# Hash attention and an MLP mixer on one core: two hashes moved at the start of the first pair

## The chip, the core and the metric

One core of a Trainium2 chip. The metric is the device time of one execution in microseconds; a median is taken over the executions of a version. "Before" is the kernel as it was, "changed" the one with the diff below.

## The reference, cut to what matters

```python
q_bits = (np.einsum('bhsd,dk->bhsk', q, proj) > 0)       # 6 sign bits per query, k the same
mask = q_bucket[:, :, :, None] == k_bucket[:, :, None, :]
scores = np.where(mask, scale * np.matmul(q, k.transpose(0, 1, 3, 2)), -1e9)
attn = exp(scores - max) / (sum + 1e-9)
x = np.matmul(attn, v)                                     # 4 batches, 8 heads, 768 tokens, 64 columns
u = x + token_mlp(x)                                       # [cut]
out = u + channel_mlp(u)                                   # [cut]
```

Only the attention matters here. Heads are handled in pairs, 16 pairs in all, and each pair in two halves of 384 queries.

## The kernel before

The hash is a matmul of q or k with the projection, then a sign. Instead of masking, the kernel adds to each score a product of the sign bits that is zero where all bits agree and hugely negative where one differs. So each block of scores takes q and k matmuls first, then a bit product into the same buffer in PSUM (where this kernel's matmuls write), then an exponential on ScalarE. The score buffers are three, and the hash of the next pair borrows one of them.

```python
def hashes(n):                        # a later pair
    g = pool.tile([P, HALF], BF16, name="g", tag="g", bufs=2)
    ps = psum.tile([P, 2, 512], F32, name="hp", tag="sc", bufs=3)[:, 0]
    # [cut] four matmuls into ps
    nc.vector.tensor_scalar(g, ps[:, :HALF], 0.0, 0.5, op0=ALU.is_gt, op1=ALU.subtract)
    nc.scalar.mul(g, g, bitscale)
    # [cut] eight DMAs from g into bitrows[n % 2]

def first_hashes(which, half):        # the first pair: straight into its place, no DMA
    # [cut] sl: the half of the tokens; to: its place in bitrows[0]
    ps = psum.tile([P, 512], F32, name="hw", tag="sm" if which else "acc", bufs=1)[:, :HALF]
    nc.tensor.matmul(ps, projwide, loaded[0][0][:, which, sl], start=True, stop=True)
    nc.vector.tensor_scalar(to, ps, 0.0, 0.5, op0=ALU.is_gt, op1=ALU.subtract)
    if which:
        nc.vector.tensor_scalar(to, to, widescale, None, op0=ALU.mult)

# in scores(), for the first half of the first pair; GR = 3, NR = 6
for c in range(NR):
    sc = psum.tile([P, 2, 512], F32, name="sc", tag="sc", bufs=3)
    product(sc, qkt, c, True)
    if first and c < GR:
        waiting.append((c, sc))
        if c == GR - 1:
            first_hashes(1, 1)
            for c, sc in waiting:
                product(sc, bits, c, False)
            for c, sc in waiting:
                exponential(sc)
        continue
    product(sc, bits, c, False)
    exponential(sc)
```

At the very start TensorE runs idle matmuls on ones while the first data arrive (`for _ in range(14)`). The main loop:

```python
for n in range(len(pairs)):
    for half in range(2):
        now = Half(n, half)
        now.scores()
        if half == 0:
            add_values(n)             # ScalarE: sum of v over tokens, rows "vt"
        now.add(0)                    # VectorE: three sums of e, rows "esd"
        # [cut] row sums of the pair before
        if half == 0 and n + 1 < len(pairs):
            hashes(n + 1)
            load_qk(n + 2)
        # [cut]
        now.add(1)
        # [cut] a step of the weight conversion
        if before:
            before.weigh()            # TensorE: e times v, rows "acc"
```

## Time and profile before

| | before |
|---|---|
| median of the first three runs | 846.69 us (846.1 to 848.8) |
| span of the profiled execution | 844.8 us |
| TensorE busy | 835.2 us, 99% |
| first hash matmul starts | 4.89 us |
| first score matmul starts | 6.34 us |
| first weighted product ("acc") starts | 22.24 us |

A timeline row gives the start in us, the duration of the merged instructions, engine, source line, operation, output<-input, shapes and count; in brackets stands the idle time just before and what ended it. A row of waits gives engine and group that waited, what for, the total in us, the number of waits and the longest. Ends of matmuls are modelled, so distances from start to start are the safer measure. The distance from the first score matmul to the first weighted product is the ruler of this document: 22.24 - 6.34 = 15.90 us before. It spans everything that the change touches, and nothing of the start-up. Its rows, with the first hash:

```profile
4.89 1.53 PE L319 MATMUL hw<-qk,projs 128*128 128x384 f32 x4 [0.78 <-DMA qk<-in_qk]
6.34 2.21 PE L340 MATMUL sc<-qk 64*128 64x384 f32 x12
...
22.24 4.09 PE L388 MATMUL acc<-e,vn 128*64 128x384 f32 x24
```

The prediction shows the rows that matter. One more row of VectorE's timeline of before belongs to it, the first sum of the second pair, with the slack in front of it:

```profile
29.03 0.96 DVE L376 SCALAR_TENSOR_TENSOR esd<-e 128x768 f32<-128x768 f32 x1 [2.06 <-ACT e L347]
```

VectorE stood idle for 2.06 us until ScalarE had made the second pair's first exponentials. Whatever arrives earlier on TensorE and ScalarE has this much room before VectorE is in the way.

### The profile page before, as it was taken

Reading aid. Unit: us, or ns where it says so; the run is one execution under the profiler, and the core shown is the slowest. Engines: PE = TensorE matmul, PEld = TensorE weight load, DVE = VectorE, ACT = ScalarE, POOL = GpSimd, SP = SyncE. Lnnn points to the kernel's source line nnn. Section 1 sums busy time; section 2 is a strip of 40 time slices with the busy share of each in tenths; the row PEclk is TensorE's granted clock in tenths of the full one; section 3 lists DMA queues with packets and bytes.
Section 4 is the critical chain, followed back from the end, with each engine's and each line's share of the span. In section 5 each row is a group of like instructions: output and inputs, shape, how many; then the busy total and the mean of one; then the engine's idle time right before and its main releaser. Section 6 shows DMA issues by size and latency. Waiting matters only on the chain.

```text
span 844.8 us, 9068 instructions
## 1 busy us (share of the span) xinstructions
PE 835.2 (99%) x3449; PEld 384.8 (46%) x3449; DVE 532.3 (63%) x652; ACT 318.7 (38%) x492; POOL 52.0 (6%) x55
## 2 busy tenths in 40 slices
PE   8999999999999999999999999999999999999997
PEld 4444444444444444555444444444444444444444
DVE  4789898998988677796564674435365432336411
ACT  4787788887888772121112101011110002111000
POOL 1000000000000000000011102001110201001110
PEclk9999999999999999999999999999999999999999
DMA  4345354455523227631012101321211110000001
GB/s 154 120 135 183 137 154 138 162 177 165 152 78 116 78 81 206 230 119 38 0 38 74 37 29 35 137 86 38 75 37 62 38 67 9 0 0 1 25 26 53
DMA packets 48755, 73.74 MB, mean 87 GB/s; under 512 B 27769, under 2 KB 29505, under 8 KB 48705
## 3 DMA queue, kind: packets, MB, share of 16 engines
q1 hardware_dynamic: 48144, 72.49, 26.2%
q8 instruction: 29, 0.48, 0.2%
q10 hardware_dynamic: 560, 0.61, 0.2%
q14 instruction: 22, 0.17, 0.1%
HBM read 59.85 MB, written 12.58 MB: 86 GB/s over the span
## 4 chain that ended last, share of the span: by engine, by line
PE 98%; DVE 1%; DMA 0%; ACT 0%; issue 0%; DVEq 0%; ACTq 0%
PE b L691 51%; PE sc L340 19%; PE acc L388 15%; PE t L616 5%; PE t L635 5%; PE sums L412 1%; PE hp L301 1%; DMA qk<-in_qk 0%; PE hw L319 0%; DVE esd L380 0%; ACT e L347 0%; DVE esd L376 0%; ACT g L306 0%; DVE bits L321 0%; DVE u L777 0%
## 5 line engine op out<-in xcount | busy, mean ns | idle before, releaser
L340 PE MATMUL sc<-qk 64*128 64x384 f32 x768 | 158.6, 492 | 2.4 <-DVE g L305 1.5
L698 ACT COPY p<-b 128x512 f32<-128x512 f32 x72 | 42.2, 586 | 307.7 <-PE b L691 307.7
L347 ACT ACTIVATE e<-sc 128x768 f32<-128x768 f32 x192 | 152.9, 812 | 14.0 <-PE sc L340 13.2
L388 PE MATMUL acc<-e,vn 128*64 128x384 f32 x768 | 130.9, 490 | 0.0
L380 DVE TENSOR_TENSOR esd<-esd,e 128x768 f32<-128x768 f32 x128 | 122.3, 955 | 10.3 <-ACT e L347 0.5
L691 PE MATMUL b<-r,WC 128*128 128x512 f32 (+1 forms) x300 | 125.6, 575 | 0.0
L691 PE MATMUL b<-T,SW 128*128 128x512 f32 x216 | 96.6, 592 | 0.0
L340 PEld LDWEIGHTS sc<-qk 64*128 64x128 f32 x768 | 66.5, 187 | 58.1 <-issue 44.9
L691 PEld LDWEIGHTS b<-r,WC 128*128 128x128 f32 x300 | 57.0, 190 | 67.1 <-issue 63.6
L388 PEld LDWEIGHTS acc<-e,vn 128*64 128x64 f32 x768 | 52.3, 137 | 74.9 <-issue 74.3
L691 PE MATMUL b<-T,WC 128*128 128x512 f32 x144 | 67.7, 592 | 0.0
L721 DVE TENSOR_TENSOR r<-p,u 128x512 f32<-128x512 f32 x18 | 12.5, 692 | 86.5 <-ACT u L698 86.5
L691 PE MATMUL b<-XT,WC 128*128 128x512 f32 x144 | 64.7, 592 | 0.0
L691 PEld LDWEIGHTS b<-T,SW 128*128 128x128 f32 x216 | 41.0, 190 | 51.7 <-issue 50.0
L340 PE MATMUL sc<-bits 64*128 64x384 bf16 x384 | 62.9, 323 | 0.0
L691 PE MATMUL b<-r,SW 128*128 128x512 f32 x144 | 62.8, 592 | 0.0
L717 POOL TENSOR_TENSOR p<-p,p 128x512 f32<-128x512 f32 x18 | 22.8, 1267 | 639.2 <-ACT p L698 628.4
L698 ACT COPY u<-b 128x512 f32<-128x512 f32 x24 | 14.1, 586 | 79.1 <-PE b L691 79.1
L691 PEld LDWEIGHTS b<-T,WC 128*128 128x128 f32 x144 | 27.4, 190 | 34.4 <-issue 34.4
L691 PEld LDWEIGHTS b<-r,SW 128*128 128x128 f32 x144 | 27.4, 190 | 34.4 <-issue 34.0
L691 PEld LDWEIGHTS b<-XT,WC 128*128 128x128 f32 x144 | 27.3, 190 | 34.1 <-issue 33.8
L616 PE MATMUL t<-x,W 128*128 128x512 f32 x96 | 41.8, 593 | 0.0
(85 smaller groups left out, 755.2 us busy)
## 6 DMA issues: line engine op xcount, KB each, us to landing
raw<-in_moe_w_ch SPq DMA_DIRECT2D x16, 768.0 KB
seen<-in_qk SPq DMA_DIRECT2D x16, 768.0 KB
qk<-in_qk SPq DMA_DIRECT2D x15, 768.0 KB
vn<-in_v SPq DMA_DIRECT2D x16, 384.0 KB
vt<-in_vT SPq DMA_DIRECT2D x16, 384.0 KB
bounced<-stage SPq DMA_DIRECT2D x32, 192.0 KB
x<-bounced SPq DMA_DIRECT2D x4, 1536.0 KB
out<-p SPq DMA_DIRECT2D x18, 256.0 KB
```

Source lines behind the costliest of these rows:

```text
L301: nc.tensor.matmul(ps[32 * j : 32 * j + 32, :HALF], projblk, loaded[n][0][:, j % 2, sl], start=True, stop=True,)
L340: nc.tensor.matmul(sc[:, i, :HALF], t[rows, 1, P * c : P * c + P], t[rows, 0, qs], start=start, stop=not start,)
L347: nc.scalar.activation(e, sc[:, :, :HALF], ACT.Exp, scale=SCALE)
L380: nc.vector.tensor_tensor(self.d, self.d, e, op=ALU.add)
L388: nc.tensor.matmul(acc[D * i : D * i + D], vn[:, i, c], e[:, i], start=(c == 0), stop=(c == NR - 1),)
L412: nc.tensor.matmul(ps[at : at + 32], ones[:, :32], self.halves[h].d[:, i], start=True, stop=True,)
L616: nc.tensor.matmul(ps, W1[:, r, P * j : P * j + P], x[:, r], start=(r == 0), stop=(r == NR - 1),)
L635: nc.tensor.matmul(ps[:, :HALF], r1[:, j, P * cb : P * cb + P], W2[:, j, HALF * half : HALF * half + HALF], start=(j == 0), stop=(j == NJ ...
L691: nc.tensor.matmul(self.ps[i][:, cols], left(k), right(k)[:, cols], start=first and k == ks[0], stop=k == ks[-1], skip_group_check=True,)
L698: nc.scalar.copy(c, self.ps[i])
L717: nc.gpsimd.tensor_tensor(p7, p5, p7, op=ALU.add)
L721: nc.vector.tensor_tensor(r[:, 3], p7, u, op=ALU.add)
```

## The change

The first move lets the first exponentials start without waiting for a hash that only the fourth block needs. The second takes the second pair's hash, on VectorE and ScalarE, out from behind sums that nobody waits for yet.

```diff
                     if first and c < GR:
                         waiting.append((c, sc))
                         if c == GR - 1:
-                            first_hashes(1, 1)
                             for c, sc in waiting:
                                 product(sc, bits, c, False)
-                            for c, sc in waiting:
                                 exponential(sc)
+                            first_hashes(1, 1)
                         continue
@@
                 now.scores()
+                if half == n == 0:
+                    hashes(1)
                 if half == 0:
                     add_values(n)
@@
-                if half == 0 and n + 1 < len(pairs):
+                if half == 0 and 0 < n < len(pairs) - 1:
                     hashes(n + 1)
+                if half == 0:
                     load_qk(n + 2)
```

## The prediction

> **What bounds the kernel now.** I read the page first, for the engine that fills the span and for the slices in which it is not full; then the waits of the tensor engine alone, because they say how much there is to win; then the chain of waits and the timelines of TensorE, VectorE and ScalarE for the first 45 us, because all of the change runs there. The page says:
>
> ```profile
> PE 835.2 (99%) x3449; PEld 384.8 (46%) x3449; DVE 532.3 (63%) x652; ACT 318.7 (38%) x492; POOL 52.0 (6%) x55
> ...
> PE   8999999999999999999999999999999999999997
> ...
> PE 98%; DVE 1%; DMA 0%; ACT 0%; issue 0%; DVEq 0%; ACTq 0%
> ```
>
> TensorE carries 98% of the chain that ends last. Only the first and the last slice are below 9. The waits of TensorE over the whole execution are four rows:
>
> ```profile
> PE sc L340 <- DVE g L305: 1.5, 1, 1.5
> PE idle L450 <- DVE ones L97: 1.0, 1, 1.0
> PE sc L340 <- ACT e L347: 0.9, 2, 0.6
> PE hw L319 <- DMA qk<-in_qk: 0.8, 1, 0.8
> ```
>
> The second and fourth are the start-up before the first hash at 4.89 us and are not touched. The other two, 2.4 us in three places, all lie between 10 and 20 us; after that TensorE waits for nothing. Ends of matmuls are modelled, so I also measure these gaps from start to start. One block of scores (four matmuls on q and k, two on bits) is issued every 0.81 us when nothing holds it, as 11.48 to 12.29 shows below; its bit part takes 0.17 of that, from 12.12 to 12.29.
>
> ```profile
> 8.48 0.91 PE L319 MATMUL hw<-qk,projs 128*128 128x384 f32 x2
> 9.33 0.66 PE L340 MATMUL sc<-bits 64*128 64x384 bf16 x6
> 10.57 0.92 PE L340 MATMUL sc<-qk 64*128 64x384 f32 x4 [0.58 <-ACT e L347]
> 11.32 0.33 PE L340 MATMUL sc<-bits 64*128 64x384 bf16 x2
> 11.48 0.81 PE L340 MATMUL sc<-qk 64*128 64x384 f32 x4
> ...
> 12.12 0.33 PE L340 MATMUL sc<-bits 64*128 64x384 bf16 x2
> 12.29 0.81 PE L340 MATMUL sc<-qk 64*128 64x384 f32 x4
> ...
> 13.19 0.91 PE L319 MATMUL hw<-qk,projs 128*128 128x384 f32 x2
> 14.03 0.85 PE L301 MATMUL hp<-qk,projs 128*32 128x384 f32 x8
> 14.81 0.92 PE L340 MATMUL sc<-qk 64*128 64x384 f32 x4
> ...
> 18.21 0.92 PE L340 MATMUL sc<-qk 64*128 64x384 f32 x4 [1.51 <-DVE g L305]
> ...
> ```
>
> The issue gaps are then: 9.33 + 3 x 0.17 = 9.84 to 10.57, 0.73 us; 14.81 + 2 x 0.81 = 16.43 to 18.21, 1.78 us; 18.21 + 0.81 = 19.02 to the fourth block's 19.62, 0.60 us. Together 3.1 us, which no version of this change can exceed. The reason for the two later ones stands in the other two timelines:
>
> ```profile
> 14.61 0.95 DVE L376 SCALAR_TENSOR_TENSOR esd<-e 128x768 f32<-128x768 f32 x1
> 15.67 2.02 DVE L380 TENSOR_TENSOR esd<-esd,e 128x768 f32<-128x768 f32 x2
> 17.60 0.55 DVE L305 TENSOR_SCALAR g<-hp 128x384 bf16<-128x384 f32 x1
> ```
>
> ```profile
> 14.03 0.84 ACT L292 ACTIVATE vt<-vt 128x768 f32<-128x768 f32 x1
> ...
> 18.25 0.62 ACT L306 ACTIVATE g<-g,bitscale 128x384 bf16<-128x384 bf16 x1 [3.30 <-DVE g L305]
> 18.77 4.41 ACT L347 ACTIVATE e<-sc 128x768 f32<-128x768 f32 x6
> ```
>
> The second pair's sign step g sits on VectorE behind three additions of e (14.61 to 17.69), though its matmuls end near 14.9. Its PSUM tile is one of the three score buffers, so the third score block of half 1 cannot start until g has read it (18.21). ScalarE's scaling of g stands before the exponentials of half 1, so they start at 18.77 and the fourth score block, which needs the first one's buffer, at 19.62.
>
> [...] ScalarE stood still for 3.30 us before g while two finished score blocks were waiting for their exponentials. [...] The trace has 812 and 602 to 616; I use the trace's start-to-start times. [...] the largest here is 1.78 us and the clock granted is 1.00 in every stretch of the first 65 us, so I give the clock no share in the gain.
>
> **The change part by part.** No instruction is added or removed; two things move.
>
> *Part 1*, the second half of the key bits. Before, its matmuls (8.48, 0.85 us to the next start) hold up the first three bit products. Now these start at 8.48 and the hash follows at 8.48 + 0.51 = 8.99. The first exponential, 9.70 before, starts 0.85 earlier at 8.85, and the first buffer is free about 0.85 later, near 9.7. So the fourth block's q and k matmuls start when the hash is through, 8.99 + 0.85 = 9.84, no longer at 10.57. But its bit product needs the key bits of that late hash. VectorE took them 0.95 us after the start of the hash (8.48 to 9.43) and was done at 10.35, 1.87 after it. Now that is 8.99 + 1.87 = 10.86; with the 0.1 us that a wait for VectorE and the weights takes, the bit product starts near 10.96. Without a wait it would start at 9.84 + 0.64 = 10.48, so a new wait of 0.5 us appears. Against 11.32 the gain is 0.35 us, not the 0.73 of the gap removed. From there TensorE sets the pace (0.81 a block against 0.72 an exponential), so hash, second pair's hash and half 1 move by 0.35: 12.84, 13.68 and 14.46.
>
> *Part 2*, g ahead of the sums. The second pair's hash matmuls start at 13.68. VectorE can read them 0.89 us later (a later pair: matmuls at 31.98, g at 32.87), at 14.57, and is done at 15.12. ScalarE starts 0.10 later, as 18.15 to 18.25 did, at 15.22; the sum of vt follows after 0.52 (the distance from 18.25 to 18.77), at 15.74, and now lies between g and the exponentials instead of in ScalarE's idle time. It holds them up by 0.82 (32.13 to the next start at 32.95). So the exponentials of half 1 start at 16.56 rather than 18.77, 2.21 us sooner. The third block starts unhindered at 14.46 + 1.62 = 16.08, since g has read its buffer at 15.12; the fourth at 16.56 + 0.85 = 17.41, after a wait of 0.5 us. The gap of 1.78 is gone; that of 0.60 stays at 0.5.
>
> *Sum.* By start times: the first weighted product, 22.24 before, starts near 20.05. By gaps: 3.1 before, 0.5 + 0.5 after, 2.1 us won. I take 2.15 us, of which 0.35 is part 1 and 1.8 is part 2. Since TensorE waits for nothing from 20 us to the end, its earlier start should reach the end whole: 846.69 - 2.15 = 844.5 us.
>
> **The rivals.** (a) VectorE becomes the bound. Its sums of the first half now start near 15.1 instead of 14.61, and its backlog moves little: five additions per half take 5.1 us, so it is done with half 0 near 20.2, with half 1 near 25.4 and with the weight conversion's two steps (1.54 us) near 26.95. The second pair's first exponentials then ask for it at 29.03 - 2.2 = 26.85. Before, it sat idle for 2.06 us there; that slack is now spent to the last tenth. Against this rival: TensorE needs the sums of half 1 only near 29.2 (31.31 - 2.15), and later rows show VectorE idle again (0.8 us before g at 32.87). If I have missed a microsecond of VectorE work, up to 1 us is given back: 845.5. (b) The bits' transfers. The eight issues took 6.09 us from 18.89 and move with g to about 15.9, ending near 22.0; the second pair's first bit product moves only from 27.01 to 24.85. Its margin grows from 2.0 to 2.9 us. I see no new wait there. (c) The new wait in part 1 is longer than reckoned, say 0.9 instead of 0.5, and part 1 gains nothing: 844.9. If the wait is short and both remaining gaps shrink, 3.1 us is the most: 843.6. (d) The time saved is lost to a transfer that has a time of its own. The loads of the third pair stand behind the bits on the same queue and so come sooner as well; nothing speaks for this. All 2.15 us lost would be 846.7.
>
> **Range and chances.** Two thirds of the weight lie at 2.0 to 2.4 us of gain. The three runs before spread over 2.7 us (846.1 to 848.8), more than the whole effect, and skewed upward, so the range is mostly that of the runs: 843.4 to 846.3. A change of 2% would be 17 us; the gaps hold 3.1. Faster by over 2%: 0.01; within: 0.98; slower: 0.01, for an order that brings a wait into every pair, which I don't see since the later pairs keep theirs.
>
> **What would show it.** In the profile after: the wait of TensorE for g is gone from its list; a wait of about 0.5 us for the key bits (VectorE, widescale row) appears at the fourth block near 10.9; the exponentials of half 0 start near 8.85 and of half 1 near 16.6; ScalarE's 3.30 us idle before g shrinks to about 1.4; the fourth block of half 1 starts near 17.4, the first weighted product near 20.05; VectorE's 2.06 us idle before the second pair's sums is nearly gone, while the first conversion step starts almost where it did (25.4). The prediction is wrong if the first weighted product is well away from 20.05, or if it is there and a new TensorE wait after 20 us gives the gain back.

No term of the sum is cut: it comes to 0.35 + 1.8 = 2.15 us won, and 846.69 - 2.15 = 844.5 us, as it stands. 812 is the mean of one exponential over 768 columns and 602 to 616 the duration of g's scaling, both in ns and from the trace before; "the largest here" is the largest issue gap. The 0.1 us for a wait for VectorE is the author's estimate: in the trace before, TensorE and ScalarE started 0.06 and 0.10 us after g was done (18.15 to 18.21 and to 18.25).

## The result, and the profile after

The median was 845.91 us (844.12 to 846.87, six runs) against 847.53 us for the kernel before (846.04 to 848.80, six runs). The ratio is 0.9978, with a 95% interval of 0.996 to 0.9996; a ratio here is the mean time of one kernel's runs over that of the other's in the same rounds, so it is not quite the ratio of the medians. 844.5 was predicted with a range of 843.4 to 846.3. The profiled execution took 846.24 us, with a span of 844.5 us: only 0.3 less than before. At first sight the gain of 2.15 us is not there. First the waits of TensorE over the whole execution of the changed kernel:

```profile
PE idle L449 <- DVE ones L97: 1.0, 1, 1.0
PE hw L319 <- DMA qk<-in_qk: 0.7, 1, 0.7
PE sc L340 <- ACT e L347: 0.3, 1, 0.3
PE sc L340 <- DVE bits L323: 0.2, 1, 0.2
```

The wait of 1.5 us for g is gone, as foreseen, the waits for ScalarE have shrunk from 0.9 to 0.3, and the new wait for the key bits is there. There is none after 20 us. So the gaps closed, and yet the span hardly moved. TensorE's timeline in the same trace shows why:

```profile
4.91 2.90 PE L319 MATMUL hw<-qk,projs 128*128 128x384 f32 x4 [0.67 <-DMA qk<-in_qk]
7.74 3.09 PE L340 MATMUL sc<-qk 64*128 64x384 f32 x12
10.67 0.65 PE L340 MATMUL sc<-bits 64*128 64x384 bf16 x6
11.25 0.91 PE L319 MATMUL hw<-qk,projs 128*128 128x384 f32 x2
12.10 0.92 PE L340 MATMUL sc<-qk 64*128 64x384 f32 x4
13.17 0.34 PE L340 MATMUL sc<-bits 64*128 64x384 bf16 x2 [0.16 <-DVE bits L323]
...
19.66 0.92 PE L340 MATMUL sc<-qk 64*128 64x384 f32 x4 [0.29 <-ACT e L347]
...
22.29 4.09 PE L387 MATMUL acc<-e,vn 128*64 128x384 f32 x24
```

The first hash began at 4.91 us, as before (4.89), but its four matmuls took 2.83 us to the first score matmul instead of 1.45, and the twelve score matmuls and their first bit product followed 2.93 us later instead of some 2.1. The same instructions ran at half rate until somewhere near 9.6 us. From the first score matmul the first weighted product is 22.29 - 7.74 = 14.55 us away, 1.35 less than before even with half-rate matmuls in that stretch. Whether the half rate comes from the change or from the execution is the question for the experiments.

ScalarE's timeline of the same execution, to be held against the three rows of before in the prediction:

```profile
17.48 0.61 ACT L306 ACTIVATE g<-g,bitscale 128x384 bf16<-128x384 bf16 x1 [1.47 <-DVE g L305]
18.00 0.83 ACT L292 ACTIVATE vt<-vt 128x768 f32<-128x768 f32 x1
...
18.82 4.41 ACT L347 ACTIVATE e<-sc 128x768 f32<-128x768 f32 x6
```

ScalarE's idle time before g shrank from 3.30 to 1.47 us (about 1.4 predicted), and the sum of vt now stands between g and the exponentials and delays them by 18.82 - 18.00 = 0.82 us.

### The profile page after: what moved, and what is told of

Same layout as the page of the kernel before. It is cut to its first block, busy times and chain, and to the rows that moved or that the text cites. A ratio compares the mean times of both kernels' runs of the same rounds, so it can differ in the third digit from the quotient of the medians. Undisturbed runs are those within 1.5% of the kernel's fastest.

```text
span 844.5 us, 9070 instructions
## 1 busy us (share of the span) xinstructions
PE 837.3 (99%) x3449; PEld 385.9 (46%) x3449; DVE 532.4 (63%) x652; ACT 318.6 (38%) x492; POOL 51.8 (6%) x55
## 4 chain that ended last, share of the span: by engine, by line
PE 98%; DMA 0%; ACT 0%; DVE 0%; issue 0%; ACTq 0%
PE b L693 51%; PE sc L340 19%; PE acc L387 15%; PE t L618 5%; PE t L637 5%; PE sums L411 1%; PE hp L301 1%; PE hw L319 1%; DMA qk<-in_qk 0%; ACT vt L292 0%; ACT e L347 0%; ACT g L306 0%; DVE g L305 0%; DVE bits L321 0%; DVE u L779 0%
```

## The experiments

Twelve runs. Those with "16" have two more idle matmuls at the start, those with "one idle matmul" have thirteen fewer.

### 1. The changed kernel once more

No edit.

> The changed kernel itself, unchanged, timed again. Theory A (the two moves save about 2.1 us of TensorE gaps; apart from that each execution, of either kernel, starts its score matmuls with TensorE at full or at half rate by chance, worth about 2.2 us): the times of both kernels fall into two groups about 2.2 us apart, before near 846.2 and 848.5, changed near 844.3 and 846.3, and the lower groups differ by 1.8 to 2.3 us. Rival B (the change itself makes the half-rate start): the kernel before has no slow group of its own, or the changed kernel shows only half-rate starts. Rival C: the spread is smooth noise without groups.

Measured: 843.91, 844.23, 844.23, 844.31, 844.36 and 846.58 us; the kernel before in the same rounds 845.72 to 846.62 (four runs) and 848.06 to 848.83 (seven). TensorE's timeline of this execution:

```profile
4.87 1.53 PE L319 MATMUL hw<-qk,projs 128*128 128x384 f32 x4 [0.61 <-DMA qk<-in_qk]
6.32 2.21 PE L340 MATMUL sc<-qk 64*128 64x384 f32 x12
8.36 0.66 PE L340 MATMUL sc<-bits 64*128 64x384 bf16 x6
8.95 0.91 PE L319 MATMUL hw<-qk,projs 128*128 128x384 f32 x2
9.79 0.92 PE L340 MATMUL sc<-qk 64*128 64x384 f32 x4
10.87 0.34 PE L340 MATMUL sc<-bits 64*128 64x384 bf16 x2 [0.16 <-DVE bits L323]
...
17.36 0.92 PE L340 MATMUL sc<-qk 64*128 64x384 f32 x4 [0.29 <-ACT e L347]
...
19.98 4.09 PE L387 MATMUL acc<-e,vn 128*64 128x384 f32 x24
```

The same kernel, and now the first hash takes 1.45 us to the first score matmul. The ruler reads 19.98 - 6.32 = 13.66 us, 2.24 less than before. So the half-rate start belongs to the execution and not to the kernel: both kernels have fast-group and slow-group runs. Over all, 25 of 48 runs of the kernel before lie at 845.66 to 846.89 (mean 846.25) and 23 at 847.67 to 849.03 (mean 848.43). Of 12 runs of the changed kernel 7 lie at 843.91 to 844.52 (mean 844.24) and 5 at 845.62 to 846.87 (mean 846.30). Lower group against lower group the change is worth 2.0 us, upper against upper 2.1. The two medians of the first comparison mixed the groups in different shares (two of six lower runs after, three of six before), which is why they differ by 1.6 only.

### 2. Each move alone

```diff
 # part1: only the first move        # part2: only the second move
-first_hashes(1, 1)                  +if half == n == 0:
 products of bits, exponentials      +    hashes(1)
+first_hashes(1, 1)                   add_values(n), sums
```

> The first move alone: second half of the key bits hashed behind the first three bit products. Theory A: 0.35 us in the timeline (fourth block's bit product about 6.1 us after the start of the first hash in a full-rate start, where before has 6.43), and the gap before the third block of half 1 stays at 1.8 us; in time about 846 in the fast group. Rival: the new wait for the key bits eats all of it, 0.0 us.

> The second move alone: the second pair's sign step and scaling ahead of the sums. Theory A: 1.8 us in the timeline (first weighted product about 15.5 us after the start of the first hash in a full-rate start, where before has 17.35), no TensorE wait for g; fast group about 844.6. Rival: it depends on the first move and gives clearly less than 1.8, say 1.2.

| | first score matmul | first weighted product | ruler | gain | times |
|---|---|---|---|---|---|
| before | 6.34 | 22.24 | 15.90 | | |
| first move | 6.17 | 21.66 | 15.49 | 0.41 | 845.57 to 846.04, five runs |
| second move | 6.02 | 20.10 | 14.08 | 1.82 | 844.17 to 844.65 (four), 847.01, 847.02 |
| both | 6.32 | 19.98 | 13.66 | 2.24 | 843.91 to 844.52 (seven), 845.62 to 846.87 (five) |

0.41 + 1.82 = 2.23: the moves add up, and each is what the prediction gave it (0.35 and 1.8). The rivals (0.0 for the first, 1.2 for the second) fall. The expectation for the first move counted from the first hash, 6.1 us to the fourth block's bit product; that was 10.72 - 4.60 = 6.12.

### 3. What the half-rate start hangs on

```diff
-        for _ in range(14):
+        for _ in range(1):      # and range(16) in the runs with 16
             nc.tensor.matmul(idle[:D, :D], ones, ones, start=True, stop=True)
```

> The changed kernel with one idle matmul at the start instead of fourteen. Theory A: every execution starts at half rate, so there is one group only, no run near 844.3; the score matmuls of the first block take about twice as long from 4.9 us to at least 8 us, and the times lie [...] 846.0 to 847.7. Rival (the half-rate start has nothing to do with how long TensorE was busy before): the same two groups as the changed kernel, 844.3 and 846.3.

Changed kernel, one idle matmul: 845.51 to 846.58 us, five runs, none near 844.3. Two runs lie below the range expected, the lowest by 0.5; that range was the author's estimate. The hash took 2.83 us in the trace, and 3.11 us followed to the first bit product.

> The kernel before with one idle matmul instead of fourteen, so that it always starts at half rate, as the changed kernel with one did (845.51 to 846.58, median 846.13). Theory A: one group, 2.2 us above that, median near 848.3, the same as the slow group of the kernel before (848.0 to 848.9); in the trace the first hash's matmuls at 2.83 us to the first score matmul instead of 1.45, and from 12 us on the distances of the first profile. Rival (the slow group comes from somewhere else, such as a drop of the rate in the idle stretch of 1.8 us): times clearly above 849.5, or two groups again.

Kernel before, one idle matmul: 847.89, 848.07, 848.25, 848.33, and then 849.57 and 850.03. The first four are what theory A said, mean 848.14 against 846.08 of the changed kernel: 2.06 us, in executions that all have the short warm-up (the two profiles reach full rate at different times, though; the table below has 9.81 and 8.15 us). The last two are a miss, and the profiled execution was one of them (849.57). Its TensorE timeline, around the stretch that the change closes:

```profile
5.07 2.90 PE L319 MATMUL hw<-qk,projs 128*128 128x384 f32 x4 [3.59 <-DMA qk<-in_qk]
...
19.86 0.92 PE L340 MATMUL sc<-qk 64*128 64x384 f32 x4 [1.51 <-DVE g L305]
20.61 0.33 PE L340 MATMUL sc<-bits 64*128 64x384 bf16 x2
21.27 1.17 PE L340 MATMUL sc<-qk 64*128 64x384 f32 x4 [0.33 <-ACT e L347]
22.23 0.54 PE L340 MATMUL sc<-bits 64*128 64x384 bf16 x2
22.55 1.50 PE L340 MATMUL sc<-qk 64*128 64x384 f32 x4
23.83 0.54 PE L340 MATMUL sc<-bits 64*128 64x384 bf16 x2
```

And its stretches (columns after the stretch: its length, busy us and count of PE, PEld, DVE, ACT and POOL, then the granted clock, DMA share and GB/s):

```profile
15.00:20.00 5.00, 3.49 (x24) 1.30 (x26) 3.99 (x6) 1.71 (x4) 0.00 (x0) 1.00 0.00 0
20.00:25.00 5.00, 4.67 (x22) 2.32 (x24) 4.47 (x5) 4.03 (x6) 0.00 (x0) 0.68 0.03 8
```

From one bit product to the next it is 1.60 us (22.23 to 23.83), twice the 0.81 of full rate, and the granted clock is 0.68 on average from 20 to 25 us. So the rival named in the expectation is real too, though not the main thing: soon after TensorE had waited for 1.51 us and again for 0.33 (the brackets above), it fell back to half rate in this profiled run, and the time of the other run at 850.03 fits it.

> The changed kernel with 16 idle matmuls instead of 14. Theory A2: no run in the group near 846.4; all between 843.8 and 845.6, so about 2.2 us below the kernel before with 16. Rival: the two groups of the changed kernel, 844.3 and 846.4, remain.

> The kernel before with 16 idle matmuls at the start instead of 14. Theory A2 (in the traces so far TensorE was at full rate from its first score block where the pause between the idle matmuls and the first hash was 0.3 to 0.6 us long or the rate had changed before that pause, and at half rate until about 9.5 us where the pause was 0.67 us and nothing had changed before it): two more idle matmuls take 0.45 us, the pause shrinks to at most 0.35 us, and the slow group at 848.0 to 848.8 disappears; all runs lie between 845.7 and 847.8. Rival (the start-up rate is pure chance, whatever TensorE does before): as many runs near 848.4 as before, about half.

Changed kernel with 16: 843.59 to 844.48, five runs, no upper group. Kernel before with 16: 845.63 to 847.08, five runs, none in the upper group, though 847.08 lies between the two. The mean goes from 845.10 (12 runs with 14) to 844.03, and from 847.29 (48 runs) to 846.24. Both expectations held, but for the lowest runs, which lie 0.2 and 0.1 below the edges given. That chance alone kept ten runs in a row out of the upper groups is unlikely: with the shares of lower runs seen with 14 (7 of 12 and 25 of 48), about 1 in 400. The means mix different chips and rounds; against the kernel before in the same rounds, the ratio of the kernel before with 16 is 0.9987 (0.9973 to 1.0001), which is not clear of 1.

The packed trace keeps records of TensorE's clock, one for each change (no view of the profile prints them; their effect is in the clock column of a table of stretches). The first record of full rate in each profiled execution, and the pause between the last idle matmul and the first hash (as shown in the brackets of its row; none where it has no bracket):

| execution | idle matmuls | pause, us | full rate from, us | hash to first score matmul, us |
|---|---|---|---|---|
| before | 14 | 0.78 | 3.82 | 1.45 |
| second move alone | 14 | 0.41 | 3.90 | 1.46 |
| changed, again | 14 | 0.61 | 4.80 | 1.45 |
| first move alone | 14 | 0.34 | 4.85 | 1.57 |
| before, second look | 14 | 0.51 | 6.23 | 2.19 |
| changed, first profile | 14 | 0.67 | 9.58 | 2.83 |
| changed, one idle matmul | 1 | 3.31 | 9.81 | 2.83 |
| before, one idle matmul | 1 | 3.59 | 8.15, lost 21.80 to 25.22 | 2.83 |
| changed, 16 | 16 | 0.22 | 4.14 | 1.46 |
| before, 16 | 16 | none | 6.54 | 2.30 |
| before, first look | 14 | 0.44 | 3.95 | 1.46 |
| latevt (experiment 4) | 14 | 0.64 | 9.68 | 2.83 |
| mid (experiment 4) | 14 | 0.82 | 3.84 | 1.46 |
| all together (experiment 5) | 16 | 0.17 | 7.12 | 2.58 |

The lost stretch is 25.22 - 21.80 = 3.42 us long. Of the starts with 14 idle matmuls, the two that reached full rate last had pauses of 0.67 us (full rate from 9.58, the first profile of the changed kernel) and 0.64 us (9.68, latevt); the five with pauses of 0.34 to 0.61 us had it from 3.90 to 6.23 us. Where the rate had gone up before the pause began, a pause of 0.78 or 0.82 us did no harm: full rate from 3.82 and 3.84 us, the last idle matmul ending at 4.11 and 4.12 (modelled ends), and the hash in 1.45 and 1.46 us. Two more idle matmuls lengthen their row from 3.25 us (changed, again) to 3.68 us (before, 16). With 16 the pause is at most 0.22 us in the profiles, and the latest full rate seen there, in three profiles, is at 7.12 us.

What decides when the rate goes up is not shown beyond this. The length of the pause alone does not order the table (0.34 us and 4.85, 0.41 and 3.90, 0.51 and 6.23), and no run varied it by itself. Nor is it shown what decides a loss: in five other profiles (before, its two looks, before with 16, the first move alone) TensorE waited for 1.51 and 0.33 us at the same two places and kept its rate, with a block of scores every 0.80 or 0.81 us right after.

> The kernel before, profiled once more, to catch its slow group. Theory A2: if the time is near 848.4, the score matmuls run at half rate from the first hash to about 9 to 10 us, and everything after is that of the first profile, shifted by about 2.2 us. Rival: TensorE is at full rate from the start and the 2.2 us lie elsewhere, such as after the idle stretch of 1.8 us before the third block of half 1. If the time is near 846.3, nothing is learned.

> The same once more, for a second chance of a slow execution of the kernel before; expectations as for the first look.

The two looks took 846.38 and 846.88 us, so neither caught the upper group; the first teaches nothing. The second has full rate from 6.23 us, between the two cases. With 14 idle matmuls, no profile shows an upper-group execution of the kernel before. It may be a late full rate, a loss after the idle stretch at 18 us, or both in turn: this stays open.

### 4. What holds TensorE after the change

```diff
 # latevt                                     # mid
-if half == 0:                                 for c, sc in waiting:
+if half == (1 if n == 0 else 0):                  product(sc, bits, c, False)
     add_values(n)                                 exponential(sc)
                                              +    if c == 0:
                                              +        first_hashes(1, 1)
                                              -first_hashes(1, 1)
```

> The changed kernel with the first pair's sum of v on ScalarE moved behind the exponentials of half 1. Theory A (that sum stands between the scaling of g and those exponentials and holds the fourth score block of half 1 back): exponentials of half 1 start 0.8 us earlier, TensorE no longer waits for ScalarE at that block, first weighted product 0.45 us earlier counted from the start of the score matmuls (13.2 us after it instead of 13.66). Rival (another releaser sets that wait, such as VectorE's reading of the hash buffer): the wait stays and the distance stays 13.66.

> The changed kernel with the key bits' second half hashed after the first bit product instead of after all three. Theory A (the fourth block waits for VectorE's two steps on that hash, 1.9 us after the hash starts): hash starts 0.4 us earlier, the wait of about 0.45 us at the fourth block's bit product shrinks to about 0.1, first weighted product about 13.3 us after the start of the score matmuls instead of 13.66. Rival: delaying the second exponential costs as much as the shorter wait gains, 13.66 again.

The first takes the sum of vt out from between g and the exponentials. Times: 843.52, 843.66, 843.85 and 845.21, 845.22, 845.45. The profile fell in the upper group (full rate from 9.68 us), so the ruler is taken from the late key hash, which all profiles run at full rate: 11.29 to the first weighted product at 21.76, 10.47 us, against 8.95 to 19.98, 11.03 us, in the changed kernel. The gain is 0.56 us (0.45 expected), and TensorE's wait for ScalarE is gone from its list. The rival, VectorE's reading of the hash buffer, falls.

The second puts the hash between the first and the second bit product. In TensorE's timeline of it:

```profile
8.44 0.33 PE L340 MATMUL sc<-bits 64*128 64x384 bf16 x2
8.70 0.91 PE L319 MATMUL hw<-qk,projs 128*128 128x384 f32 x2
9.54 0.50 PE L340 MATMUL sc<-bits 64*128 64x384 bf16 x4
9.88 0.81 PE L340 MATMUL sc<-qk 64*128 64x384 f32 x4
10.62 0.34 PE L340 MATMUL sc<-bits 64*128 64x384 bf16 x2
10.79 0.91 PE L340 MATMUL sc<-qk 64*128 64x384 f32 x4
11.53 0.33 PE L340 MATMUL sc<-bits 64*128 64x384 bf16 x2
11.69 0.81 PE L340 MATMUL sc<-qk 64*128 64x384 f32 x4
```

The fourth block's bit product comes 0.74 us after its q and k matmuls (9.88 to 10.62), where the changed kernel took 1.08 (9.79 to 10.87). So the theory holds: the later the hash, the longer that wait. From the first score matmul this bit product is 10.62 - 6.40 = 4.22 us away instead of 10.87 - 6.32 = 4.55, 0.33 sooner. But the ruler reads 19.83 - 6.40 = 13.43, a gain of 0.23 only; 0.36 was expected. The tenth is lost at the fifth block: the sixth follows it after 0.90 us (10.79 to 11.69) instead of 0.81. That fits the rival in part: the second exponential, now from 9.92 to 10.73, frees the fifth block's buffer; that block's weight loads begin at 10.78, only 0.01 us before its matmuls, where the changed kernel has 0.17 (10.87 to 11.04). No releaser is named for these loads, so this is an argument and not shown. Times: 843.67 to 844.26 (four runs), 845.39, 846.51.

### 5. All together

The changed kernel with 16 idle matmuls and both edits of experiment 4.

> The changed kernel with all three: 16 idle matmuls, the key bits' second half hashed after the first bit product, the sum of v behind the exponentials of half 1. If the gains add up (0.56 and 0.23 us in the timelines, and no slow group): first weighted product 12.9 us after the start of the score matmuls instead of 13.66, TensorE has no wait of 0.1 us or more after the first hash, all runs between 842.8 and 844.2, median near 843.2. Rival (the two waits shadow each other): 13.1 to 13.4 us, median near 843.7.

Measured: 843.40, 843.59, 843.60, 843.65 and 844.41, the last one 0.2 above the range expected; median 843.60, 0.4 above the expected 843.2 and nearer to the rival's 843.7; in the same rounds 847.81 for the kernel before (845.94 to 848.91, nine runs), ratio 0.9956 (0.9943 to 0.9970). The waits of TensorE over the whole execution are down to the start-up:

```profile
PE idle L450 <- DVE ones L97: 1.0, 1, 1.0
PE hw L319 <- DMA qk<-in_qk: 0.2, 1, 0.2
```

The ruler reads 20.30 - 7.43 = 12.87 us, which is 13.66 - 0.56 - 0.23. In the timeline the gains add up, and no wait of TensorE after the first hash is left in the list. In the times they don't show whole: the median is 0.4 below that of the changed kernel with 16 (843.99), where the ruler says 0.79. The profiled execution, at 844.41, lost 1.13 us to a late full rate (first hash 2.58 us instead of 1.45); whether the other four lost some in the same way is not known. Its ratio is the lowest, and its interval overlaps that of the changed kernel with 16 (0.9950 to 0.9978).

## Why the prediction was right or wrong

The mechanism held to about a tenth of a microsecond, once an execution with the same start is taken. In the changed kernel's second profile (first hash at 4.87, before 4.89):

| step | predicted, us | measured, us |
|---|---|---|
| exponentials of half 0 start | 8.85 | 8.73 |
| fourth block's bit product | 10.96 | 10.87 |
| new wait for the key bits, reckoned alike | 0.5 | 10.87 - 9.79 - 0.64 = 0.44 |
| exponentials of half 1 start | 16.56 | 16.52 |
| fourth block of half 1 | 17.41 | 17.36 |
| first weighted product | 20.05 | 19.98 |
| first conversion step on VectorE | 25.4 | 25.22 |
| sum won | 2.15 | 2.24 |

The two starts of the exponentials in that profile:

```profile
8.73 2.21 ACT L347 ACTIVATE e<-sc 128x768 f32<-128x768 f32 x3 [5.60 <-PE sc L340]
...
16.52 4.41 ACT L347 ACTIVATE e<-sc 128x768 f32<-128x768 f32 x6
```

One reading was too large, without harm: the prediction's gaps count every block as 0.81 us, but its own rows show 0.92 for the first block after the hash (14.81 to 15.73), so the gap of 1.78 is 15.73 + 0.81 = 16.54 to 18.21, 1.67 us, and the total 3.0, not 3.1 (experiment 5, with no wait left, won 15.90 - 12.87 = 3.03). The forecast of 20.05 was summed from start times and does not rest on it.

*Part 1* is right: the new wait takes about half of what the move frees (0.41 us are left, measured alone). *Part 2* is right: 1.82 against 1.8. *The gain reaches the end*: no wait of TensorE after 20 us appeared in either profile of the changed kernel, from the first weighted product to the end of the span it took 822.2 and 822.1 us against 822.6 before (821.9 to 822.6 in all fourteen profiles), and lower group against lower group the time fell by 2.0 us.

Rival (a), VectorE as the bound, was close and did not bite. In VectorE's timeline of the changed kernel's second profile, the slack of 2.06 us is spent and the first sum of the second pair follows the conversion at once:

```profile
25.22 0.55 DVE L177 TENSOR_SCALAR tmp<-raw 128x768 uint32<-128x768 uint32 x1
25.81 0.96 DVE L180 SCALAR_TENSOR_TENSOR tmp<-raw,tmp 128x768 uint32<-128x768 uint32 x1
26.77 0.96 DVE L375 SCALAR_TENSOR_TENSOR esd<-e 128x768 f32<-128x768 f32 x1
```

Rival (b), the transfers of the bits, shows no wait in the lists of TensorE, so it is out as well; (c) is out by experiment 2, and (d) because lower group against lower group nearly all of the gain is there.

The step that failed is the sentence on the clock: "so I give the clock no share in the gain". It rested on a granted clock of 1.00 in every stretch and on taking gaps of up to 1.78 us for harmless, which no run had shown. Both readings were too simple. The row of the clock showed 1.00 for the changed kernel's first 5 us and the next as well, while its matmuls ran at half rate: the row is right only from the first record of a change on, and that was at 9.58 us. Its stretches (columns as in experiment 3; 1.00 is the clock):

```profile
0.00:5.00 5.00, 3.33 (x29) 3.18 (x29) 0.11 (x1) 1.28 (x1) 3.28 (x19) 1.00 0.57 177
5.00:10.00 5.00, 5.00 (x12) 2.43 (x14) 1.44 (x3) 0.00 (x0) 0.00 (x0) 1.00 1.02 406
```

And the loss in experiment 3 came after two waits of 1.51 and 0.33 us, in the places of the gaps of 1.78 and 0.60 us. For the mean gain this mattered little, since both kernels pay for a late start (with one idle matmul their first hash took 2.83 us in both, and they lay 2.06 us apart in experiment 3); for the range it mattered a good deal. The three runs before (846.1, 846.69, 848.8) were read as noise that is "skewed upward", when they were two from one group and one from the other. The predicted 844.5 is the lower group of the changed kernel (843.91 to 844.52); the median of 845.91 is one of a mixture. The range of 843.4 to 846.3 held the median, but it was right about the spread without knowing its cause, and that was luck in part: the base of 846.69 was a lower-group time, the same kernel's median over six runs was 847.53, and the changed kernel's six runs gave 845.91 once and 844.27 the next time, by how many fell into the upper group.

One consequence was not foreseen at all: by closing the stretch of 1.8 us the change also takes away the place in which a fall back to half rate was seen. It was seen in one profile, of the kernel before with a shorter warm-up; how often it happens in the kernel before as it stands was not shown.

## What to carry to other kernels

When one engine is at 99%, list its few real waits, measure them from start to start, and work out for each move what it frees and what new wait it makes; here such a sum came out within 0.1 us. A small instruction that releases a shared buffer, or that stands first in another engine's order, belongs in front of work that nobody waits for yet; here g was both, and moving it won 1.82 us. If the repeated times of a kernel fall into groups, find what the groups are before comparing medians: one profile of each kernel can put 2 us of chance on either side (the means of the groups lay 2.06 and 2.18 us apart here), and a ruler that starts after the start-up is free of it (from the late key hash to the first weighted product, 11.04 and 11.03 us in the changed kernel's two profiles, one with the half-rate start and one without). See whether idle matmuls that warm up TensorE last until its real work can start: with two more of them here, and a pause of at most 0.22 us left, none of ten runs lay in an upper group.
